# Attention scores of two heads in the two 64-row halves of TensorE, masks in VectorE's maxima, a padded last block

## The chip, the cores and the metric

One core of a Trainium2 chip runs the whole program. The metric is the device time of one execution in microseconds (us); several executions are timed and the median counts.

## The reference

Four sequences (B) of 576 positions (S) with eight heads (H) of 64 numbers (D) go through causal attention mixed with a memory read. The 2304 rows that come out are routed to eight experts of at most 288 rows each, and then go through a second feed-forward layer. The change touches the attention alone:

```
scores = scale * np.matmul(q, k.transpose(0, 1, 3, 2))      # q, k: (4, 8, 576, 64)
scores = np.where(causal, -1000000000.0, scores)
scores = scores - scores.max(-1, keepdims=True)
a = np.exp(scores)
a /= a.sum(-1, keepdims=True) + 1e-09
local = np.matmul(a, v)
...
mem_out = mem_ret / mem_norm
return (g * mem_out + (1 - g) * local).astype(np.float32)
...
x = np.ascontiguousarray(attn_out.transpose(0, 2, 1, 3)).reshape(B * S, H * D)
x = _moe_ref(x=x, **moe_kwargs)
return _moe2_ref(x=x, **moe2_kwargs)
```

## The kernel before, in words

The program has three stages, one after the other: attention, routing, and the experts with the second layer. Attention works on 16 pairs of heads (`pair(p)`: sequence `p // 4`, heads `2 * (p % 4)` and the next). Rows of 576 positions are cut into five blocks of 128, 128, 128, 128 and 64.

A number is held as a rounded high part and the low part that is left over, so that products come out nearly in full precision.

For each pair:

- Loads: K and Q with the 64 numbers of a head on partitions and both heads side by side (`Kr`, and `Qr`, which is loaded twice, into both halves of the partitions); Q in its natural layout, head 0 on partitions 0 to 63 and head 1 on 64 to 127 (`QN`); V, its transpose `VT`, and the memory `MZ`.
- Splitting: ScalarE casts `KX` (high), `QX` (high, twice) and `KB` (all of K); VectorE subtracts to get K's low part, into the lower half of `KX`, and Q's low part, `QL`. Each of these runs over 1152 columns.
- S, to find row maxima: `piece` multiplies a block of queries by the keys up to it (one matmul of 128 rows holds high and low parts of K), after a small matmul with `identb` and `mask_s` that puts a large negative number over the future keys (line 394 and then 396). For the last 64 queries, `QJ` holds both heads side by side with zeros between, and two matmuls (line 400) add up. VectorE reduces each piece to a maximum (line 413). These run about one pair ahead.
- nm: the ten columns of maxima are turned by a matmul (line 440), copied, and written by three small DMAs on ScalarE's queue (`fn3`, lines 449 and 450) into row 64 of `QL`.
- T, the scores again with keys on the output's partitions, so that they can feed the next product: `tprod` makes each block with two matmuls, K's high and low parts by Q's high part (line 555, 128 rows) and all of K by Q's low part with the row of minus the maxima (line 556, 65 rows). One head at a time; three groups of 512 columns a head, and the last 64 keys of both heads in a fourth group. ScalarE takes the exponential into `PT` (line 575), GpSimd zeroes the future keys on the diagonal (line 605).
- AV: `fAV` multiplies `PT` by V block by block into one buffer `av` (line 591), 15 blocks a head. In query block 4 the last product has 64 rows of `PT`. These matmuls are plain fp32, and each shows as two passes in the trace.
- mem (line 510) and the gate's product g0 (line 463) go through another single buffer; VectorE scales and adds (`norm`).

Beside this, 24 pieces of the last layer's weights are unpacked on ScalarE and VectorE (`conv`).

The order of the work on each engine is fixed when the program is built: `Plan.run` takes the tasks, each with a due number, an estimated length and the buffers it needs, and always places the task that can start first, by its estimates. Engines run their instructions strictly in that order, so an instruction that waits holds up all that stands behind it on its engine; DMA issues of SyncE's queue (SP) likewise. Rings limit how far things run ahead: S has three PSUM buffers, T two, `av` one.

Of the kernel before, what the change touches and what calls it, by code (L numbers as in the profile page):

```python
# [17 lines left out]
try:  # L18
# [36 lines left out]
BUFS = {"Kr": 2, "Qr": 2, "QN": 2, "MZ": 2, "V": 3, "VT": 2, "phi": 1, "ph": 1, "KX": 3, "QX": 3, "QL": 2, "KB": 2, "QJ": 2, "nm": 2,  # L55
        "nmt": 2, "PT": 2, "s": 3, "t": 2, "r5": 2, "tmp": 1, "rm": 2, "x": 2, "g": 2, "m2raw": 1, "m2a": 1, "m2b": 1}
OFFK = (0, 576, 1024, 1344, 1536)
MASK = -8.0e9
PRIO = {"load": -24, "prep": -18, "cb": 8, "S": -14, "ds": 1.2, "N": -5, "nmte": "ACT", "G": -3, "phi": -6, "mem": (1.6, 6.6), "memx": "ACT",
        "T": (0.5, 2.2, 3.5), "A": 5, "norm": 14, "gate": 6, "m2": (0.0, 6.3, 8.0), "tmg": (1, 6, 9, 12)}  # L60
VW, GW = 112, 112


C = 73
COLD, NLAT = 6000, 2600
# [32 lines left out]
class Ring:  # L98
    def __init__(self, n):
        self.n, self.made = n, []  # L100
# [14 lines left out]
class Plan:  # L115


    def __init__(self, cold=0):
        self.tasks, self.wrote, self.read, self.cold = [], {}, {}, cold
# [24 lines left out]
    def run(self):  # L144
# [7 lines left out]
        while len(order) < len(self.tasks):  # L152
            best, hold, cands = None, {}, []
            for t in ready:
# [7 lines left out]
                for e, c in t.engs.items():  # L162
# [7 lines left out]
                    st = max(at, free.get(e, 0), now)  # L170
# [58 lines left out]
def attention(g, tc, ctx, consts, beta, qT, kT, qN, v1, vT, mz, mT, wg, xd, L, m2):  # L229
# [10 lines left out]
    warm = cs.tile([128, 512], BF, name="warm")  # L240
    V.memset(warm, 0.0)
    zero = cs.tile([128, 192], F32, name="zero")
    G.memset(zero, 0.0)
    ms = cs.tile([128, 192], BF, name="mask_s")
    G.affine_select(ms[:, :128], zero[:, :128], pattern=[[-1, 128]], compare_op=OP.is_ge, fill=MASK, base=0, channel_multiplier=1)
    for i in range(2):
        q = slice(64 * i, 64 * i + 64)
        G.affine_select(ms[q, 128:], zero[q, :64], pattern=[[-1, 64]], compare_op=OP.is_ge, fill=MASK, base=0, channel_multiplier=1)
    identr = cs.tile([128, 128], F32R, name="identr")
    identb = cs.tile([128, 128], BF, name="identb")  # L250
    V.tensor_copy(identr, g.ident)
    V.tensor_copy(identb, g.ident)
# [7 lines left out]
    plan = Plan(COLD)  # L260
# [16 lines left out]
    def tile(name, shape, dt=F32):  # L277
        return (ld if name in ("Kr", "Qr", "QN", "MZ", "V", "VT") else wk).tile(shape, dt, name=name, bufs=BUFS[name])

# [12 lines left out]
    KB = [cs.tile([65, 2, S], F32R, name=f"KB{k}") for k in range(BUFS["KB"])]  # L292
    QJ = [cs.tile([128, 4, 64], F32R, name=f"qj{k}") for k in range(BUFS["QJ"])]
    for t in QJ:
        V.tensor_copy(t[:, 1:3].rearrange("p a b -> p (a b)"), zero[:, :128])
    tkb = []
    for k, t in enumerate(KB):
        def f(e, t=t):
            V.tensor_scalar(t[64:65, 0], warm[64:65, :256].bitcast(F32)[:, :1].to_broadcast([1, S]), 0.0, -1.0, op0=OP.mult, op1=OP.add)
            V.tensor_copy(t[64:65, 1], t[64:65, 0].bitcast(F32))  # L300

        tkb.append(add(10 * k - 7, {"DVE": 730}, f))
# [4 lines left out]
    def pair(p):  # L307
# [3 lines left out]
        bf = r.b = {x: Buf(R[x]) for x in ("Kr", "Qr", "QN", "MZ", "V", "VT", "phi", "ph", "KX", "QX", "QL", "KB", "QJ", "nm", "nmt",  # L311
                                           "PT", "av", "r5", "tmp")}
        parts = [(0, 1), (1, 2)] if p == 0 else [(0, 2)]
        k0 = n + W["load"]

        def load(name, shape, src, key, ns, a=None, z=None, dup=1, first=True):
            def f(e):
                if first:
                    setattr(r, name, tile(name, shape))
                t = getattr(r, name)  # L320
                for x in range(dup):
                    d = t[64 * x:64 * x + 64] if dup > 1 else t
                    nc.sync.dma_start(d if a is None else d[:, a:z], src if a is None else src[:, a:z])
            return add(key, {"SP": ns}, f, new=[bf[name]] if first else [], use=[] if first else [bf[name]])

        tK, tQ = [], []
        for u, (a, z) in enumerate(parts):
            tK.append(load("Kr", [64, 2, S], kT[b, pp], k0 - 3 * (p == 0) + .01 * u, 1400 // len(parts), a, z, 1, u == 0))
            tQ.append(load("Qr", [128, 2, S], qT[b, pp], k0 - 3 * (p == 0) + .011 * u + .001, 2200 // len(parts), a, z, 2, u == 0))
        tN = load("QN", [128, S], qN[b, pp], k0 + .1, 1200)  # L330
# [6 lines left out]
        tck, tcq, tsk, tsq, tcb = [], [], [], [], []  # L337
        for u, (a, z) in enumerate(parts):
            k, w = kp + .5 * u, S * (z - a)
            s = slice(a, z)  # L340

            def ck(e, s=s, u=u):
                if not u:
                    r.KX = tile("KX", [128, 2, S], F32R)
                copy(e, r.KX[:64, s], r.Kr[:, s])

            def cq(e, s=s, u=u):
                if not u:
                    r.QX = tile("QX", [128, 2, S], F32R)
                copy(e, r.QX[:, s], r.Qr[:, s])  # L350

            def sk(e, s=s):
                V.tensor_sub(r.KX[64:, s], r.Kr[:, s], r.KX[:64, s].bitcast(F32))

            def sq(e, s=s, u=u):
                if not u:
                    r.QL = tile("QL", [65, 2, S], F32R)
# [1104 lines left out]
```

## Time and profile before

| | us |
|---|---|
| median of 3 runs | 884.77 (881.39 to 887.12) |
| the profiled execution | 890.54, its span 888.8 |
| TensorE busy in the span | 842.4 (95%) |
| attention, to the last AV product | about 285 |
| routing | about 285 to 340 |
| experts and second layer | the rest |

The engines are TensorE (PE; PEld is its loading of weights), VectorE (DVE), ScalarE (ACT), GpSimd (POOL) and SyncE's queue (SP). A row of the timeline gives the start in us, the length, engine, line, operation, tile written <- tiles read, the weights' rows*columns, the shape of the moving data, and after x how many instructions or passes of one kind follow each other. TensorE overlaps neighbouring matmuls, so the length of one is not what it costs: the cost is from its start to the next one's start. A row of a line's instructions gives shortest/median/longest length in ns and then the first and the last start in us. A row of groups gives the line, the shapes and count, then the busy us and the mean ns of one.

### The profile page before, as it was taken

Reading aid. Unit: us, or ns where it says so; the run is one execution under the profiler, and the core shown is the slowest. Engines: PE = TensorE matmul, PEld = TensorE weight load, DVE = VectorE, ACT = ScalarE, POOL = GpSimd, SP = SyncE. Lnnn points to the kernel's source line nnn. Section 1 sums busy time; section 2 is a strip of 40 time slices with the busy share of each in tenths; the row PEclk is TensorE's granted clock in tenths of the full one; section 3 lists DMA queues with packets and bytes.
Section 4 is the critical chain, followed back from the end, with each engine's and each line's share of the span. In section 5 each row is a group of like instructions: output and inputs, shape, how many; then the busy total and the mean of one; then the engine's idle time right before and its main releaser. Section 6 shows DMA issues by size and latency. Waiting matters only on the chain.

```text
span 888.8 us, 17312 instructions
## 1 busy us (share of the span) xinstructions
PE 842.4 (95%) x6750; PEld 780.6 (88%) x6750; DVE 578.3 (65%) x1487; ACT 365.7 (41%) x826; POOL 96.8 (11%) x200
## 2 busy tenths in 40 slices
PE   8999999999998479979999999999999999999997
PEld 6888988888886379969999999999999999999996
DVE  7588888778874879957775775674586462542421
ACT  4667777667655223313412412412421432432311
POOL 1121112113111010113002002002001001000001
PEclk9999999999999579989999999999999999999999
DMA  8756776855630231252402421431330441430000
GB/s 215 176 153 178 222 200 183 227 159 163 186 93 24 92 108 49 81 113 68 149 25 69 127 47 52 143 49 48 133 72 28 142 73 30 140 72 25 25 1 37
DMA packets 39619, 92.87 MB, mean 104 GB/s; under 512 B 11184, under 2 KB 13360, under 8 KB 39536
## 3 DMA queue, kind: packets, MB, share of 16 engines
q1 hardware_dynamic: 36240, 82.24, 33.8%
q0 software_dynamic: 2976, 9.44, 3.2%
q8 instruction: 53, 0.87, 0.5%
q14 instruction: 30, 0.25, 0.1%
q10 hardware_dynamic: 320, 0.07, 0.0%
HBM read 82.21 MB, written 9.45 MB: 103 GB/s over the span
## 4 chain that ended last, share of the span: by engine, by line
PE 58%; issue 22%; DVE 5%; ACT 5%; DMA 4%; ACTq 2%; POOL 2%; SPq 1%; POOLq 0%; DVEq 0%
PE w L1204 8%; PE w L1206 8%; PE w L1205 8%; PE av L591 7%; PE acc L1205 4%; PE acc L1204 4%; PE acc L1206 4%; PE t L555 2%; PE mem L463 2%; DMA xg<-xd,tidx 2%; PE t L556 2%; PE s L396 2%; ACT x L533 2%; PE mem L510 2%; PE rps L953 1%
## 5 line engine op out<-in xcount | busy, mean ns | idle before, releaser
L1204 PE MATMUL w<-yh,mh 128*128 128x288 f32 x576 | 174.1, 302 | 0.0
L1206 PE MATMUL w<-yh,ml 128*128 128x288 f32 x576 | 169.9, 295 | 0.0
L1205 PE MATMUL w<-yl,mh 128*128 128x288 f32 x576 | 169.5, 294 | 0.0
L591 PE MATMUL av<-V,PT 128*128 128x112 f32 (+2 forms) x960 | 118.8, 263 | 1.3 <-DVE tmp L642 1.0
L591 PEld LDWEIGHTS av<-V,PT 128*128 128x128 f32 (+2 forms) x960 | 107.2, 173 | 8.9 <-issue 0.9
L1204 PEld LDWEIGHTS w<-yh,mh 128*128 128x128 f32 x576 | 108.8, 189 | 2.8
L1205 PEld LDWEIGHTS w<-yl,mh 128*128 128x128 f32 x576 | 108.5, 188 | 3.0
L1206 PEld LDWEIGHTS w<-yh,ml 128*128 128x128 f32 x576 | 108.4, 188 | 0.0
L1174 DVE TENSOR_TENSOR wlo<-wraw,whi 128x1024 fp32r<-128x1024 f32 x64 | 78.2, 1223 | 38.1 <-ACT whi L1170 38.1
L1311 DVE TENSOR_TENSOR mt<-w,mt 128x288 f32<-128x288 f32 x96 | 43.6, 455 | 81.6 <-PE w L1206 76.1
L1170 ACT CAST whi<-wraw 128x1024 fp32r<-128x1024 f32 x64 | 66.7, 1048 | 37.8 <-PE acc L1205 19.0
L413 DVE TENSOR_REDUCE nm<-s 128x1 fp32r<-128x512 f32 (+4 forms) x160 | 72.4, 475 | 14.5 <-PE s L400 6.4
L1205 PE MATMUL acc<-hl,whi 128*128 128x288 f32 x256 | 76.0, 297 | 1.4 <-DVE hl L1111 0.9
L1204 PE MATMUL w<-xhi,whi 128*128 128x288 f32 x256 | 77.2, 302 | 0.0
L1206 PE MATMUL w<-xhi,wlo 128*128 128x288 f32 x256 | 76.7, 299 | 0.1
L1205 PE MATMUL w<-xlo,whi 128*128 128x288 f32 x256 | 76.7, 300 | 0.0
L1072 ACT CAST gc<-mt 128x32 fp32r<-128x32 f32 (+2 forms) x72 | 17.5, 243 | 143.6 <-DVE mt L1311 138.9
L1204 PE MATMUL acc<-hh,whi 128*128 128x288 f32 x256 | 76.2, 297 | 0.0
L575 ACT ACTIVATE PT<-t 128x512 f32<-128x512 f32 x96 | 57.6, 601 | 43.5 <-PE t L556 28.6
L1206 PE MATMUL acc<-hh,wlo 128*128 128x288 f32 x256 | 75.2, 294 | 0.0
L1137 POOL DMA_INDIRECT xg<-xd,tidx x24 | 27.1, 1130 | 377.2 <-PE w L1206 181.5
L1111 DVE SCALAR_TENSOR_TENSOR hl<-w,hh 128x288 fp32r<-128x288 f32 x64 | 29.2, 456 | 59.0 <-ACT hh L1105 54.3
(219 smaller groups left out, 1802.9 us busy)
## 6 DMA issues: line engine op xcount, KB each, us to landing
wraw<-in_wr SPq DMA_DIRECT2D x64, 512.0 KB
Qr<-in_qT SPq DMA_DIRECT2D x30, 288.0 KB
m2raw<-in_m2w SPq DMA_DIRECT2D x12, 512.0 KB
V<-in_v SPq DMA_DIRECT2D x16, 365.0 KB
QN<-in_qN SPq DMA_DIRECT2D x16, 288.0 KB
VT<-in_vT SPq DMA_DIRECT2D x16, 288.0 KB
Kr<-in_kT SPq DMA_DIRECT2D x15, 288.0 KB
xd<-x SPq DMA_DIRECT2D x16, 256.0 KB
```

What stands on the lines that cost most here:

```text
L396: PE.matmul(d, r.QX[:, i, 128 * j:128 * j + 128], r.KX[:, i, a:z], start=False, stop=True, skip_group_check=True)
L413: V.tensor_reduce(r.nm[:, col:col + k], o.s[:, c:c + k * w].rearrange("p (k w) -> p k w", k=k), axis=AX.X, op=OP.max)
L575: A.activation(r.PT[:, items[0][0], out:out + 512], o.t, AF.Exp, scale=0.125)
L591: PE.matmul(AV[:m, i, j * C:j * C + w], r.PT[:kr, i, o:o + m], r.V[:kr, c:c + w], start=kb == 0, stop=kb == j)
L1111: V.scalar_tensor_tensor(lo(), src(), 0.0, hi().bitcast(F32), op0=OP.max, op1=OP.subtract)
L1137: g.gather = G.indirect_dma_start(out=x.xg[:96, c], out_offset=None, in_=xd, in_offset=bass.IndirectOffsetOnAxis(ap=r.tidx[:96, c:c + 1], ...
L1170: A.copy(x.W[fb][0], x.RAW[fb])
L1174: V.tensor_sub(x.W[fb][1], x.RAW[fb], x.W[fb][0].bitcast(F32))
L1204: nc.tensor.matmul(o, wh, rh, start=start, stop=False)
L1205: nc.tensor.matmul(o, wh, rl, start=False, stop=False)
L1206: nc.tensor.matmul(o, wl, rh, start=False, stop=stop)
L1311: V.tensor_max(q.mt, o.pt[:, :T], q.mt)
```

## The change

- K is loaded in its natural layout too (`KR`: head 0 on partitions 0 to 63, head 1 on 64 to 127), and `QN` serves for Q; `Qr` and `Kr` are gone. High and low parts `KH`, `QH`, `KL`, `QL` are tiles of 128 partitions by 576, so casts and subtractions have half the columns, and `KB` is gone.
- T of both heads is made together: each block has four products (`KH` by `QH`, `KL` by `QH`, `KH` by `QL`, and a constant of -1 by `NM`, which holds the maxima in rows 0 and 64), and each is issued for head 0 on rows 0 to 63 and at once for head 1 on rows 64 to 127, into two PSUM buffers. So there are eight matmuls where two heads had four. The last 64 keys go into the tail of the buffers that the third group's S takes.
- S uses high parts alone, both heads in the two halves; the mask's matmuls are gone. VectorE adds a mask while it takes the maximum (`tensor_tensor_reduce`, which is built as two instructions: the pass itself and one that writes out its accumulator). The last 64 queries take one matmul of 128 rows by 512 and one by 64.
- S of pair p+2 is issued behind T of pair p in the same task (`AHEAD = 2`); S and T share one ring of five PSUM buffers instead of three and two.
- The maxima get a cast of their own on ScalarE (`nmr`), and the DMAs that write them stand on SP's queue among the loads.
- AV goes query block by query block for both heads; `PT` has zeros in the missing 64 rows of its last block, so every AV product has 128 rows.
- `QJ` is copied by GpSimd.

```
-BUFS = {"Kr": 2, "Qr": 2, ..., "PT": 2, "s": 3, "t": 2, ...}
+BUFS = {"KR": 2, "QN": 3, ..., "PT": 2, "st": 5, ...}
...
-        for u, (a, z) in enumerate(parts):
-            tK.append(load("Kr", [64, 2, S], kT[b, pp], ...
-            tQ.append(load("Qr", [128, 2, S], qT[b, pp], ...
+        tK = load("KR", [128, S], kN[b, pp], k0 - 3 * (p == 0), 1200)
+        tN = load("QN", [128, S], qN[b, pp], k0 - 3 * (p == 0) + .001, 1200)
...
-                    if j < 4:
-                        PE.matmul(o.s[:, c + z - a - 128:c + z - a], identb, ms[:, :128], start=True, stop=False, ...)
-                        PE.matmul(d, r.QX[:, i, 128 * j:128 * j + 128], r.KX[:, i, a:z], start=False, stop=True, ...)
+                    for i in range(2):
+                        PE.matmul(o.s[i][:, c:c + 128 * j + 128], r.QH[H2[i], 128 * j:128 * j + 128], r.KH[H2[i], :128 * j + 128],
+                                  start=True, stop=True)
...
-                    V.tensor_reduce(r.nm[:, col:col + k], o.s[:, c:c + k * w].rearrange(...), axis=AX.X, op=OP.max)
+                        V.tensor_tensor_reduce(out=junk[:, :w], in0=o.s[x][:, c:c + w], in1=m, scale=1.0, scalar=-3.0e38, op0=OP.add,
+                                               op1=OP.max, accum_out=r.nm[:, col:col + 1])
...
-                A.dma_start(q[:, i, :512], r.nmt[4 * i:4 * i + 4])
-            A.dma_start(q[:, :, 512:], r.nmt[8:9].rearrange("o (i q) -> o i q", i=2))
+            nc.sync.dma_start(q[0:128:64, :512], r.nmt[:8])
+                nc.sync.dma_start(q[64 * i:64 * i + 1, 512:], r.nmt[8:9, 64 * i:64 * i + 64])
...
-                PE.matmul(d, r.KX[:, i, ks_], r.QX[:, i, a:z], start=True, stop=False)
-                PE.matmul(d, r.KB[:, i, ks_], r.QL[:, i, a:z], start=False, stop=True)
+                    for x, (wt, mv) in enumerate(((r.KH, r.QH), (r.KL, r.QH), (r.KH, r.QL), (None, r.NM))):
+                        for q, d in zip(H2, ts):
+                            PE.matmul(d[:kr, c:c + z - a], neg[q, :kr] if wt is None else wt[q, k], mv[q, a:z], start=x == 0, stop=x == 3)
...
-                    PE.matmul(AV[:m, i, j * C:j * C + w], r.PT[:kr, i, o:o + m], r.V[:kr, c:c + w], start=kb == 0, stop=kb == j)
+                    PE.matmul(AV[:m, i, j * C:j * C + w], r.PT[:, i, o:o + m], r.V[:, c:c + w], start=kb == 0, stop=kb == j)
```

On TensorE, S and T of a pair stood in small pieces between other work. Before, in the middle of attention (t is T, s with mask_s and identb is the mask, s<-KX,QX is S, mem is the memory):

```order
L440 MATMUL s<-identr,nm 9x128 [waits DVE_49]
L555 MATMUL t<-QX,KX 128x512 [waits Activation_49]
L556 MATMUL t<-QL,KB_126 128x512 [waits DMAHW7_49]
L394 LDWEIGHTS identb
L394 MATMUL s<-mask_s,identb 128x128
L396 MATMUL s<-KX,QX 128x512
L510 MATMUL mem<-MZ,phi 128x146
```

Now, at the end of T's second group and through the third (st is the shared ring; x2 is one matmul for each half):

```order
L557 MATMUL st<-nm_129,neg 128x448 x2
L384 MATMUL st<-KH,QH 128x384 [waits DVE_49] x2
L557 MATMUL st<-QH,KH 128x320 [waits Activation_49] x2
L557 MATMUL st<-QH,KL 128x320 x2
L557 MATMUL st<-QL,KH 128x320 x2
L557 MATMUL st<-nm_129,neg 128x320 x2
L557 MATMUL st<-QH,KH 128x192 x2
L557 MATMUL st<-QH,KL 128x192 x2
L557 MATMUL st<-QL,KH 128x192 x2
L557 MATMUL st<-nm_129,neg 128x192 x2
L557 MATMUL st<-QH,KH 64x64 [waits DVE_49]
L557 MATMUL st<-QH,KH 64x64 [waits Activation_49]
```

The work of 64 rows now stands in two runs a pair: the first group with its S, and the second and third groups with theirs, back to back. The third group's first matmuls wait for ScalarE, which empties the ring's buffers.

On SP's queue the loads and, now, the maxima's DMAs (nm_128<-nmt) stand in one row, behind loads that wait for buffers (m2raw is the weights' piece to unpack, which has one buffer):

```order
L324 DMA QN<-in_qN 128x576 [waits DMAHW6_49,DVE_49]
L324 DMA V<-in_v 128x730 [waits DMAHW7_49,PE_49]
L758 DMA m2raw<-in_m2w 128x1024 [waits DMAHW0_49,DMAHW3_49,DVE_49,Activation_49]
L439 DMA nm_128<-nmt 2x4x128 [waits DMAHW1_49,Activation_49]
L441 DMA nm_128<-nmt 1x16x4 [waits DMAHW2_49]
```

Before, SP's queue held loads alone in this place, and the three DMAs stood on ScalarE's queue.

On VectorE at the end of attention (L is the gate's sums, am the first step of routing), one unpacking now stands between the last sum and routing, where before there was nothing between them:

```order
L674 TENSOR_TENSOR L<-L,lt 64x8 [waits DVE_49]
L772 TENSOR_SCALAR m2b<-m2raw 128x512 [waits DMAHW4_49,DVE_49]
L775 SCALAR_TENSOR_TENSOR m2b<-m2a,m2b 128x512 [waits DVE_49,Activation_49]
L778 SCALAR_TENSOR_TENSOR w_80<-m2raw,m2b 128x512 [waits DVE_49]
L889 TENSOR_REDUCE am<-L 128x1 [waits Pool_49]
```

The three operations of the unpacking moved behind the last sum.

## Rows read from the trace of the kernel before

**Rows 1.** Stretch of nine pairs: its length, then each engine's busy us

```profile
64.90:211.30 146.40, 143.18 (x1134) 125.44 (x1134) 122.23 (x277) 103.33 (x241) 22.61 (x56) 1.00 0.68 193
```

**Rows 2.** Line 440, one matmul a pair: all of its matmuls

```profile
L440 PE MATMUL s<-identr,nm x16: 223/227/229, 14.4 to 260.5; 128*9 128x128 f32 x16
```

**Rows 3.** Line 555, T's first matmuls: all of them

```profile
L555 PE MATMUL t<-QX,KX x192: 191/302/502, 22.0 to 276.8; 128*128 128x512 f32 x32, 128*128 128x64 f32 x32, 128*128 128x448 f32 x32, 128*128 128x320 f32 x32
```

**Rows 4.** Timeline of TensorE through one pair

```profile
112.20 0.45 PE L555 MATMUL t<-QX,KX 128*128 128x512 f32 x1
112.48 0.39 PE L556 MATMUL t<-QL,KB 65*128 65x512 f32 x1
112.72 0.23 PE L394 MATMUL s<-mask_s,identb 128*128 128x128 bf16 x1
...
113.81 0.23 PE L394 MATMUL s<-mask_s,identb 128*128 128x128 bf16 x1
...
114.16 0.19 PE L555 MATMUL t<-QX,KX 128*128 128x64 f32 x1
...
114.79 2.38 PE L591 MATMUL av<-V,PT 128*128 128x112 f32 x20
117.01 0.22 PE L394 MATMUL s<-mask_s,identb 128*128 128x128 bf16 x1
...
117.30 0.31 PE L555 MATMUL t<-QX,KX 128*128 128x320 f32 x1
...
117.60 0.26 PE L555 MATMUL t<-QX,KX 128*128 128x192 f32 x1
...
117.90 0.99 PE L591 MATMUL av<-V,PT 128*64 128x73 f32 x10
...
119.81 0.23 PE L394 MATMUL s<-mask_s,identb 128*128 128x128 bf16 x1
...
120.24 0.65 PE L591 MATMUL av<-V,PT 128*128 128x112 f32 x4
...
123.11 0.35 PE L400 MATMUL s<-KX,qj 128*128 128x64 f32 x2
...
123.34 0.28 PE L555 MATMUL t<-QX,KX 128*128 128x64 f32 x1
123.46 0.28 PE L556 MATMUL t<-QL,KB 65*128 65x64 f32 x1
...
125.62 0.71 PE L400 MATMUL s<-KX,qj 128*128 128x512 f32 x2
126.17 0.31 PE L555 MATMUL t<-QX,KX 128*128 128x320 f32 x1
...
126.98 0.99 PE L591 MATMUL av<-V,PT 128*64 128x73 f32 x10
127.90 0.23 PE L440 MATMUL s<-identr,nm 128*9 128x128 f32 x1
```

**Rows 5.** Timeline: the first eight of the ten passes at 126.98

```profile
126.98 0.72 PE L591 MATMUL av<-V,PT 128*64 128x73 f32 x8
```

**Rows 6.** Timeline: the last two of them, with 64 rows

```profile
127.63 0.34 PE L591 MATMUL av<-V,PT 64*64 64x73 f32 x2
```

**Rows 7.** Timeline of line 713 in full, products into two halves of the columns

```profile
25.36 0.64 PE L713 MATMUL mem<-wb,m2raw 128*64 128x8 f32 x16
```

**Rows 8.** Groups of VectorE by shape, from 30 to 285 us

```profile
L413 DVE TENSOR_REDUCE nm<-s 128x1 fp32r<-128x512 f32 x42 | 28.7, 684 | 9.9 <-PE s L400 5.9 <-PE s L396 3.8
L353 DVE TENSOR_TENSOR KX<-Kr,KX 64x1152 fp32r<-64x1152 f32 x13 | 17.6, 1353 | 1.9 <-ACT KX L290 1.6
L436 DVE TENSOR_TENSOR nm<-nm 128x1 fp32r<-128x1 f32 x14 | 2.5, 178 | 0.3
```

**Rows 9.** The same for ScalarE

```profile
L575 ACT ACTIVATE PT<-t 128x512 f32<-128x512 f32 x92 | 55.2, 602 | 41.4 <-PE t L556 26.5 <-PE s L396 10.8 <-DMA QL<-nmt 4.0
```

**Rows 10.** Waits of SP's queue: us in total, times, longest

```profile
SPq L753 <- DVE w L773: 27.0, 14, 5.3
```

More of the change, by code (lines that the diff above doesn't have):

```diff
@@ L169, in run @@
                         at = max(at, u.end + (0 if u.eng == e else LAT[u.eng][e]))
-                    st = max(at, free.get(e, 0), now)
+                    st = max(at + self.wait * (e == "PE"), free.get(e, 0), now)
                     cands.append((t, e, c, st))
@@ new lines, in alone @@
+        def alone(o):
+            o.after(add(o.key, {"PE": o.cost + 130}, o.fn, o.deps, new=o.bs + o.first, use=o.use))
+        ks = n + W["S"]
+        r.pieces = [piece(ks + W["ds"] * a, [(j, 0)], [(i, 0, 128 * j + 128, 4 * i + j) for i in range(2)]) for a, j in enumerate((3, 2))]
+        r.pieces.append(piece(ks + W["ds"] * 2, [(1, 0), (0, 256)],
+                              [(i, c, w, 4 * i + j) for i in range(2) for j, c, w in ((1, 0, 256), (0, 256, 128))]))
+        if p < AHEAD:
+            for o in r.pieces:
+                alone(o)
@@ L559, in score @@
[L559 to L581 removed]
+        ex, mk = {}, {}
@@ L618, in pair @@
[L618 to L622 removed]
+                m = rows(kb)
+                v = r.PT[:m, :, OFFK[kb]:OFFK[kb] + m]
+                G.affine_select(v, v, pattern=[[0, 2], [1, m]], compare_op=OP.is_ge, fill=0.0, base=0, channel_multiplier=-1)
@@ new lines, in select @@
+            gi = (0, 1, 2, 2, 3)[kb]
+            mk[kb] = add(n + W["T"][min(gi, 2)] + .1 + .01 * kb, {"POOL": 100 + 2.5 * rows(kb)}, f, [ex[0, gi], ex[1, gi]], use=[bf["PT"]])
+        outs = []
+        for gi in range(3):
+            score(gi)
+        for kb in range(NJ):
+            select(kb)
+        for j in range(NJ):
+            for i in range(2):
+                need = [mk[x] for x in range(j + 1)] + ([ex[x, 1] for x in range(2)] if j == 4 else [])
+                outs.append(add(n + W["A"][j] + .5 * i, {"PE": (225, 450, 675, 900, 330)[j]}, fAV(i, j),
+                                need + outs[-2:][:1] * (j > 0) + [r.tV] + (fill if p == 0 else []), new=[bf["av"]] if not outs else [],
@@ L721, in attention, with begin @@
         tmg.append(add(W["tmg"][b] + .1, {"ACT": 156}, f1, [t], use=[bm]))
+    ahead, gens = {}, {}
+    def begin(p):
+        if p < NP:
+            gens[p] = pair(p)
+            ahead[p] = next(gens[p])
+    for p in range(AHEAD):
+        begin(p)
     for p in range(NP):
-        r = pair(p)
+        begin(p + AHEAD)
+        r = next(gens[p])
         b, pp = divmod(p, H // 2)
```

328 lines of the change are left out of this document (146 added, 182 removed).

## The prediction

> **What bounds the kernel now.** I read the busy times by stretch first. Over nine pairs in the middle of attention TensorE is busy for 143.2 of 146.4 us, VectorE for 122.2 (83%) and ScalarE for 103.3 (71%) [rows 1]: TensorE's queue sets the pace, at 146.4 / 9 = 16.3 us a pair. The rows of line 440, one matmul a pair, tell the same over nearly all of attention: 15 steps from 14.4 to 260.5, 16.4 us each [rows 2]. So a microsecond taken off TensorE's queue in one pair is worth 16 at the end, as long as nothing else falls behind. Attention ends with a chain of small steps into routing, and the later stages share nothing with the change, so I move them by whatever attention gains.
>
> Then I read one pair in the timeline, always from start to start [rows 4]. T of one head: the first group takes 0.52 (112.20 to 112.72), the second 0.63 (114.16 to 114.79), the third 0.60 (117.30 to 117.90), or 0.81 with the last 64 keys of both heads behind it (126.17 to 126.98). Two heads: 2 x (0.52 + 0.63) + 0.60 + 0.81 = 3.71. S with its masks: 0.35 for 512 columns (113.81 to 114.16), 0.29 for 384 (117.01 to 117.30), 0.43 for 256 and 128 together (119.81 to 120.24), each for two heads, and 0.23 (123.11 to 123.34) and 0.55 (125.62 to 126.17) for the last queries: 2.92. T and S are 6.63 us of a pair.
>
> **The change on TensorE.** First the price of one matmul when the next follows at once [rows 4]: 0.24 for 512 columns (112.48 to 112.72), 0.15 for 320 (two in 117.30 to 117.60), 0.12 for 64 (123.34 to 123.46; here the load of 128 columns of weights sets it). Between these I put 0.21 for 448, 0.18 for 384, 0.13 for 256 and 0.12 for 192 and 128. With 64 columns of weights: eight passes last 0.72, of which the last one's own length is about 0.22; seven steps in 0.50 make 0.07 [rows 5].
>
> If the two halves run side by side, a couple of matmuls costs what one does. T: 4 products x (0.24 + 0.12 + 0.21 + 0.15 + 0.12 + 0.07) = 3.64, about what it was. S: 0.24 + 0.18 + 0.13 + 0.12 = 0.67, and the last queries 0.28 + 0.12 = 0.40, half of what they were. Together 4.71. That a couple costs one is not shown for rows by any row of before. The nearest is line 713, whose products alternate between the two halves of the columns: sixteen passes with 64 columns of weights last 0.64, so fifteen steps take 0.42, 0.028 each [rows 7], against 0.071 in one half [rows 5]. There two halves did run at once, weights included. I take that end; the other, one after the other, is a rival.
>
> Here a measured figure of the Trainium skill ("TensorE: Matmul & The Clock Gate", Part 3, "Measured speedup vs the span model") speaks against full overlap. It gives 3.07 times for four row tiles of 512 columns, not 4; by that a couple would cost 1.30 of one, 4.31 x 0.30 x 16 = 21 us more over attention. No row here has row tiles, and line 713 shows no such loss; the rule is weighed as a rival below.
>
> Going from 128 rows to 64 and back has a price. Ten even passes of 0.071 would take 0.71; with 64 rows in the last two (they begin at 127.63 [rows 6], the next work at 127.90) the ten take 0.92 [rows 4], so 0.21 for in and out. The new order has two runs of 64 rows a pair: 0.42. At the entry the first load of weights is not hidden: the first 512-column matmul of a group takes 0.28 (112.20 to 112.48) and not 0.24, twice 0.04. T and S become 4.71 + 0.42 + 0.08 = 5.21, a gain of 1.42.
>
> The padded last block makes those two switches of AV vanish, once for each head: 2 x 0.21 = 0.42.
>
> **The new wait.** T's third group now follows the second at once, and its first matmuls wait for ScalarE to empty buffers of the ring. One exponential takes 0.60 [rows 9]; the S of 384 columns in between covers 0.18. Below: 0, if the buffer is free by chance. Above: 1.2, both exponentials in a row. I take 0.5, one exponential less its cover and something for the hand-over. Behind the waiting matmul stand the rest of T, this pair's AV and all of TensorE's queue.
>
> Net for one pair: 1.42 + 0.42 - 0.5 = 1.34; for sixteen 21.4 us.
>
> **The other engines.** VectorE loses two subtractions of 1152 columns (1.35 each) for two of 576 (about 0.68 by the 512-column reduction), -1.3 a pair; its nine masked maxima each get an instruction that writes one column, between 0 and the 0.18 of the smallest operation, up to +1.6 a pair [rows 8]. I price the masked pass itself like the reduction of the same columns. VectorE's 122.2 / 9 = 13.6 us a pair [rows 1] become 12.3 to 13.9, against 16.3 - 1.3 = 15.0 for TensorE: hidden, with little room. ScalarE sheds three casts of 1152 columns for two of 576 and three DMA issues, and gets a small cast and a second copy; at 71% busy nothing of it shows. GpSimd is busy for 22.6 of 146.4 [rows 1]; its copies of `QJ` are hidden there.
>
> On SP the maxima's three DMAs stand behind loads. The unpacking's loads waited 27.0 us in 14 times for their buffer, the longest 5.3 [rows 10]. But the maxima of a pair are turned before the second run of the pair ahead of it and are used in the next first run, over half a pair, some 8 us, later. I cost it at nothing; if a wait of 5.3 came on top of copying and landing in every pair, the excess would stop T's fourth product and with it TensorE.
>
> **Start and end.** T first starts at 22.0 us [rows 3]. S now needs no low parts, and Q comes once. But pair 0's T is followed on TensorE by S of pair 2, whose loads are issued behind pair 0's maxima. I take 2 us, between 0 and 5. At the end one unpacking stands between the last sum and routing's first reduction: three operations of 512 columns, about 0.68 each [rows 8], 2 us; 0 if it runs earlier. The two cancel.
>
> **The sum.** 21.4 us. From the profiled execution's 890.5 that gives 869; this execution was 5.8 above the median, and I take the same off the median: 884.8 - 21.4 = 863.4, say 863. With the wait at 0 and 5 us at the start: 16 x 1.84 + 5 = 34, 850. With the wait at 1.2: 16 x 0.64 = 10, 875.
>
> **The rivals.**
>
> 1. The halves run one after the other. Every couple costs two: T and S's 4.31 once more, less some 0.3 of the new wait that longer S covers, 4.0 x 16 = 64 us: 863 + 64 = 927, slower by 5%. Against it stands line 713 [rows 7]; for it, that no row shows halves of rows. It decides alone: above 1 + 21.4 / (4.31 x 16) = 1.31 of one matmul for a couple, nothing is gained.
> 2. They overlap in part, because the second half's load of weights comes behind the first's. Then 0.12 shows where few columns cover it, about 0.1 in four of T's six blocks: 4 x 0.36 = 1.4, and 0.2 in S, 1.6 x 16 = 26 us: 889, no change. Line 713 loads in both halves without loss [rows 7], which speaks against it. The Trainium skill's 3.07 of 4, named above, would end in about the same place, 884.
> 3. The couples overlap, but the ring of five buffers or VectorE, at about 87%, holds TensorE up at more places: for each run one reduction of 0.68 late, 1.4 a pair instead of part of my 0.5, about 1 us more: 863 + 16 = 879. If the masked pass took twice the reduction's time, VectorE itself would need over 16 us a pair, and this would end at no change.
> 4. The change does not do what it says, since T costs the same and most of S was hidden. I see no cover: TensorE is busy 98% [rows 1], so S's time is on the path.
>
> **Chances.** The forecast, 850 to 875: 0.68. Quicker, with no wait and a better start: 0.05. Rival 3: 0.12, a third of it below 876. Rival 2: 0.08. Rival 1: 0.07. A measurement of this kernel can tell about 1%, 9 us, from no change. Faster by more than that (below 876) is 0.68 + 0.05 + 0.04 = 0.77; within 1% the rest of rival 3 and most of rival 2, 0.15; slower 0.08. For the range I leave out rival 1, half of rival 2 and what is quicker than 848: 848 to 884 holds about 0.8.
>
> **What would show it.** Right: the matmul of the maxima recurs every 15 us; T's and S's matmuls come in couples a few ns apart and the couple with 512 columns takes 0.24; one wait of TensorE for ScalarE of about half a microsecond a pair; the AV products of query block 4 take 0.71 and not 0.92. Wrong: couples at 0.4 or more for 512 columns (rivals 1 and 2); TensorE idle for VectorE or for the maxima's DMA several times a pair, or VectorE above 95% (rival 3); T starting later than 22 us.

## The result and the profile after

| | before | changed | ratio, 95% interval |
|---|---|---|---|
| median of the comparison | 885.94 (4 runs) | 873.61 (871.64 to 874.77, 4 runs) | 0.9872 [0.9831, 0.9913] |
| again, beside e2 to e4 (e1) | 886.23 (13 runs) | 872.44 | 0.9823 [0.9764, 0.9882] |
| again, beside e13 to e15 (e16) | 887.84 (7 runs) | 874.78 | 0.9853 [0.9827, 0.9879] |
| the profiled execution | 890.54, span 888.8 | 874.77, span 873.0 | |

The kernel became faster by 12 to 14 us. Forecast were 22 us, to 863.0; the time lies inside the range of 848 to 884, and a little over half of the gain came.

In the rows below, st is a buffer of the ring that S and T share, pt the exponentials' tile, KH, KL, QH and QL the high and low parts, junk the output of the masked maximum that nobody reads. The first view is the stretch of nine pairs in the middle, which answers [rows 1], and the matmul of the maxima, which answers [rows 2]:

```profile
59.90:197.80 137.90, 131.74 (x1253) 114.33 (x1252) 109.52 (x352) 85.52 (x248) 26.44 (x72) 1.00 0.52 159
```

```profile
L430 PE MATMUL st<-identr,nmr x16: 227/228/319, 16.7 to 243.3; 128*9 128x128 f32 x16
```

A pair takes 137.9 / 9 = 15.3 us and not 16.3. TensorE's share fell from 98% to 96%: something waits now. VectorE has 12.2 us of work in a pair, ScalarE 9.5.

The timeline of TensorE, as in [rows 4], first a piece with T's first group and the last column block of AV, then the second and third group:

```profile
133.45 0.50 PE L557 MATMUL st<-QH,KH 64*128 64x512 f32 x2
133.79 0.39 PE L557 MATMUL st<-QH,KL 64*128 64x512 f32 x2
134.03 0.40 PE L557 MATMUL st<-QL,KH 64*128 64x512 f32 x2
134.26 0.39 PE L557 MATMUL st<-nm,neg 64*128 64x512 f32 x2
134.49 0.40 PE L384 MATMUL st<-KH,QH 64*128 64x512 f32 x2
134.82 0.85 PE L597 MATMUL av<-V,pt 128*64 128x73 f32 x10
135.60 1.01 PE L504 MATMUL mem<-MZ,phi 128*128 128x146 f32 x6
```

```profile
121.67 0.36 PE L557 MATMUL st<-QH,KL 64*128 64x448 f32 x2
121.87 0.36 PE L557 MATMUL st<-QL,KH 64*128 64x448 f32 x2
122.07 0.37 PE L557 MATMUL st<-nm,neg 64*128 64x448 f32 x2
122.28 0.33 PE L384 MATMUL st<-KH,QH 64*128 64x384 f32 x2
122.45 0.31 PE L557 MATMUL st<-QH,KH 64*128 64x320 f32 x1
123.89 0.41 PE L557 MATMUL st<-QH,KH 64*128 64x320 f32 x1 [1.14 <-ACT pt L583]
```

Each "x2" is a couple, one product for each head. From start to start a couple of 512 columns costs 0.23 to 0.24, of 448 columns 0.20, of 384 0.17: what one matmul cost before. The ten passes of AV's last column block take 0.78 (134.82 to 135.60), before 0.92. And here the second matmul of the third group starts 1.44 behind the first: it waits for ScalarE. Every pair has such a wait, and this is the longest: TensorE's idle time there is 1.14 in this pair and 0.36 to 0.87 in the others. ScalarE's timeline at that place:

```profile
122.01 1.34 ACT L527 ACTIVATE x<-mem,rm 128x64 f32<-128x64 f32 x6 [0.73 <-DVE g L517]
123.21 1.12 ACT L583 ACTIVATE pt<-st 128x512 f32<-128x512 f32 x2
```

The two exponentials that free the buffers stand behind six evictions of mem. Over all pairs the waits of TensorE (total, times, longest) put 9.0 us there, those of its weight loads 12.9:

```profile
PE st L557 <- ACT pt L583: 9.0, 14, 1.1
```

```profile
PEld st L557 <- ACT pt L583: 12.9, 14, 1.4
```

VectorE's groups by shape from 30 to 267 us, which answer [rows 8]: the masked maximum of 512 columns takes 690 ns, as long as the plain one (684) in [rows 8], and writing its accumulator out 83 each time.

```profile
L397 DVE CUSTOM_DVE_ANT_0 junk<-st,mask 128x512 bf16<-128x512 f32 x26 | 17.9, 690 | 13.3 <-PE st L384 11.9
L397 DVE DVE_READ_ACCUMULATOR2_ANT nm<- 128x1 f32 x124 | 10.3, 83 | 0.0
```

The start. T first runs at 25.2 us, before at 22.0 [rows 3]. TensorE, then ScalarE, then SP's queue:

```profile
23.47 1.80 PE L504 MATMUL mem<-MZ,phi 128*128 128x146 f32 x6 [2.31 <-issue]
25.20 0.79 PE L557 MATMUL st<-QH,KH 64*128 64x512 f32 x2
```

```profile
22.43 0.67 ACT L294 CAST KH<-KR 128x576 fp32r<-128x576 f32 x1 [1.66 <-DMA KR<-in_kN]
23.00 0.37 ACT L294 COPY mg<-mem 64x32 f32<-64x32 f32 x2
```

```profile
17.33 0.67 SPq L439 DMA_DIRECT2D nm<-nmt  x1
18.05 1.24 SPq L441 DMA_DIRECT2D nm<-nmt  x2
19.40 0.52 SPq L324 DMA_DIRECT2D KR<-in_kN  x1
```

Read from the end: TensorE's mem products need the single buffer that the copy of mg at 23.00 empties (the row names no releaser; this follows from the kernel, and e2 below tests it). That copy stands on ScalarE behind the cast of pair 2's K; the cast waits for the load, and the load went out at 19.40, behind the DMAs of pair 0's maxima. TensorE idles for 2.3 us, and its clock falls behind it (the column behind POOL is the granted clock; 0.50 is the lower of its two levels, 1.2 GHz):

```profile
20.00:25.00 5.00, 2.40 (x23) 2.11 (x23) 1.55 (x2) 2.31 (x8) 1.15 (x4) 0.77 0.86 267
25.00:30.00 5.00, 4.26 (x24) 3.33 (x24) 1.96 (x7) 2.36 (x8) 0.41 (x1) 0.50 0.28 104
30.00:35.00 5.00, 5.00 (x44) 3.76 (x41) 1.95 (x8) 3.55 (x9) 0.82 (x3) 0.70 0.16 34
```

The end. Between the last sums on VectorE and routing's first reduction (L889) stand three operations of the unpacking:

```profile
270.28 0.43 DVE L772 TENSOR_SCALAR m2b<-m2raw 128x512 int32<-128x512 int32 x1
270.81 0.69 DVE L775 SCALAR_TENSOR_TENSOR m2b<-m2a,m2b 128x512 int32<-128x512 int32 x1
271.54 0.69 DVE L778 SCALAR_TENSOR_TENSOR w<-m2raw,m2b 128x512 int32<-128x512 int32 x1
272.15 0.29 DVE L889 TENSOR_REDUCE am<-L 128x1 f32<-128x144 f32 x1
```

### The profile page after: what moved, and what is told of

The parts are those of the page before. It is cut to its first block, busy times and chain, and to the rows that moved or that the text cites. A ratio compares the mean times of both kernels' runs of the same rounds, so it can differ in the third digit from the quotient of the medians.

```text
span 873.0 us, 17954 instructions
## 1 busy us (share of the span) xinstructions
PE 820.9 (94%) x6958; PEld 760.7 (87%) x6958; DVE 559.1 (64%) x1628; ACT 334.5 (38%) x839; POOL 100.7 (12%) x234
## 4 chain that ended last, share of the span: by engine, by line
PE 68%; issue 22%; DVE 4%; ACT 3%; DMA 2%; POOL 2%; POOLq 0%; DVEq 0%; ACTq 0%
PE av L597 12%; PE w L1209 9%; PE w L1211 8%; PE w L1210 8%; PE st L557 6%; PE acc L1210 4%; PE acc L1209 4%; PE acc L1211 4%; PE mem L504 3%; PE mem L456 2%; DMA xg<-xd,tidx 2%; PE rps L958 1%; ACT x L527 1%; PE st L384 1%; PE av L689 1%
## 5 line engine op out<-in xcount | busy, mean ns | idle before, releaser
L597 PE MATMUL av<-V,pt 128*128 128x112 f32 (+1 forms) x960 | 111.8, 265 | 0.0
L597 PEld LDWEIGHTS av<-V,pt 128*128 128x128 f32 (+1 forms) x960 | 98.2, 173 | 12.9 <-issue 8.5
L397 DVE CUSTOM_DVE_ANT_0 junk<-st,mask 128x512 bf16<-128x512 f32 (+2 forms) x144 | 66.2, 460 | 30.1 <-PE st L384 20.4
L583 ACT ACTIVATE pt<-st 128x512 f32<-128x512 f32 x96 | 52.4, 605 | 25.1 <-PE st L557 24.2
```

The lines of the kernel that those rows point to most:

```text
L397: V.tensor_tensor_reduce(out=junk[:, :w], in0=o.s[x][:, c:c + w], in1=m, scale=1.0, scalar=-3.0e38, op0=OP.add, op1=OP.max, accum_out=r.nm ...
L583: A.activation(r.PT[:, i, 512 * gi:512 * gi + 512], o.t[i], AF.Exp, scale=0.125)
L597: PE.matmul(AV[:m, i, j * C:j * C + w], r.PT[:, i, o:o + m], r.V[:, c:c + w], start=kb == 0, stop=kb == j)
```

## The experiments

My theory after reading the traces: the couples do run at once, and the missing gain went to the start, to the wait for the ring, and to a padding that is worth less than forecast. The rivals: that VectorE or the ring's depth holds TensorE whatever ScalarE's order, that the start is bound by the maxima's transfers, and that the halves' overlap is not where T's gain comes from. Pair lengths below are those of the 13 pairs from the third to the sixteenth matmul of the maxima.

**e1: the changed kernel again**, beside the next three.

> The changed kernel once more, to set the size of the effect on a chip that runs the other kernels of this call beside it. Theory A (the two profiles differ by 15.8 us, of which 4.6 us are the profiled execution of before being above its median): ratio 0.985 to 0.989, about 12 us. Theory B (the profiles tell the true effect): 0.981 to 0.983, about 16 us.

872.44, ratio 0.9823 [0.9764, 0.9882]; a pair takes 15.30 us, and T starts at 25.1. The effect on this chip is 13.8 us by the medians, between the two theories and less than the 15.8 between the profiled spans. The interval spans both theories, so e1 doesn't decide between them.

**e2: pair 2's K and Q loaded earlier.**

```
-        tK = load("KR", ..., k0 - 3 * (p == 0), 1200)
+        tK = load("KR", ..., k0 - 3 * (p == 0) - 8 * (p == 2), 1200)
```

(and the same for `QN`.)

> The changed kernel with the loads of pair 2's K and Q issued on SP ahead of the beta, m2raw and first-row-maxima transfers instead of behind them; nothing else is changed. Theory A: the start lost about 5 us to the forecast since mem(0) waits for a copy on ScalarE that stands behind the cast of KR(2), whose load was issued only at 19.4 us; then the first T stands at 21 to 23 us instead of 25.2, TensorE's idle stretch 21.2 to 23.5 goes, and the time falls 3 to 6 us against the changed kernel. Rival: the first T is bound by the row maxima's transfers (nm), which the two loads now delay; T stays at 25 or moves later and the time is the same within 1 us or 1 to 3 us longer.

867.35 beside 872.44, 5.1 less; ratio 0.9775 [0.9719, 0.9831]. TensorE at the start, and the clock:

```profile
22.20 0.64 PE L708 MATMUL mem<-wb,m2raw 128*64 128x8 f32 x16 [0.52 <-ACT mg L294]
22.77 0.63 PE L557 MATMUL st<-QH,KH 64*128 64x512 f32 x2
```

```profile
25.00:30.00 5.00, 4.88 (x39) 4.04 (x39) 3.10 (x11) 3.12 (x10) 0.88 (x4) 0.86 0.60 220
30.00:35.00 5.00, 5.00 (x54) 4.57 (x52) 2.51 (x13) 3.73 (x12) 2.14 (x5) 1.00 0.07 18
```

T starts 2.4 us earlier, the low stretch is shorter, and the third matmul of the maxima comes at 40.4 instead of 44.2. Of the 2.4 us, 1.7 come from the planner, which with this edit puts pair 0's mem behind T's first group (at 25.04, in the changed kernel ahead of it at 23.47); the 3.7 us at the third matmul of the maxima are the fairer measure. The pairs stay at 15.31. So the start did cost 4 to 5 us, and through the place of two loads; that the maxima's transfers hold it falls, as these went out 0.1 later here. e15, below, repeats it.

**e3 and e6: the exponentials ahead of mem's evictions on ScalarE**, in the changed kernel (e3) and with the early loads (e6). In the sorted list of tasks, those evictions are moved behind the second group's exponentials:

```
+        for t in [t for t in seq if hasattr(t, "evict")]:
+            a = seq.index(t)
+            z = next((k for k in range(a + 1, min(a + 13, len(seq))) if hasattr(seq[k], "second")), None)
...
+            seq.insert(z, seq.pop(a))
```

> The changed kernel with the two exps of T's second group moved ahead of the six evictions of the second half of mem on ScalarE's queue, in 11 or more of the 16 pairs; nothing else is changed. Theory A: the ring wait in T's third group (0.8 to 1.1 us a pair) is set by those evictions, 1.34 us, that stand in front of the exps; the wait falls below 0.3 and the time falls by 0.6 to 0.9 us a pair, 8 to 13 us in all. Rival B: the wait moves on to g0, which then waits for the later evictions to free MEM; the wait in T falls but as much appears in front of g0, and the time stays within 3 us. Rival C: VectorE is what holds the ring; the wait in T stays.

> The kernel with the two early loads (e2), and the exps of T's second group ahead of the mem evictions as in e3. In e3 the pairs grew shorter by 0.16 us each, but the clock of the start rose later and took 2 us back. Theory A (what e3 lost was the clock of its start alone): no low stretch after 35 us, pairs of 15.14 us, and 1.5 to 3 us less than the kernel with the early loads, which was 0.9775 of before: 0.974 to 0.976. Rival B (exps first delays what stands behind it): the same as e2 within 1 us, 0.977 to 0.979.

e3 gave 873.58, no gain (e1: 872.44); e6 871.09, ratio 0.9796 [0.9742, 0.985]. The wait in T's third group fell in e3:

```profile
PE st L567 <- ACT pt L593: 5.5, 13, 0.4
```

But 0.4 of it stays in each pair; one exponential lasts 0.55. Pairs took 15.14 in both, 0.16 less, which makes some 2.5 us over sixteen. At the start it was lost again: the clock stood at 0.50 in e3 from 30 to 35 us, where the changed kernel had 0.70, and in e6 from 25 to 30, where e2 had 0.86, and the third matmul of the maxima came 2.0 and 1.8 us later. That this is the edit's doing isn't shown: in e16, the changed kernel again, the clock stood at 0.50 from 30 to 35 too, and that matmul came at 46.3, as in e3 (46.2). The medians can't tell 2.5 us from this. So theory A of e3 holds for the place, with a quarter of its size a pair; the evictions are the lesser part of the wait.

**e4: the padding alone, in the kernel before.**

```
-                    PE.matmul(AV[...], r.PT[:kr, i, o:o + m], r.V[:kr, c:c + w], ...)
+                    PE.matmul(AV[...], r.PT[:, i, o:o + m], r.V[:, c:c + w], ...)
```

with two fixed tiles for `PT` whose last rows are zeroed once.

> The kernel before with the padding alone: PT in two fixed buffers whose lower half of the last block is zeroed once, and AV's last block taken with 128 rows instead of 64. Theory A (the forecast's): the two switches between 128 and 64 rows per pair and head go, 0.42 us a pair, 6 to 7 us in all. Theory B (by the traces of the changed kernel, where the ten passes of the last column block take 0.78 us instead of 0.92): 0.28 us a pair, 4 to 5 us in all. Rival: the static PT takes a release order away and costs as much as it gains; within 2 us of before.

884.95 beside 886.23, ratio 0.9979 [0.9953, 1.0006]; a pair 16.31 instead of 16.37. The ten passes took 0.78 instead of 0.92, twice a pair, but TensorE waited more often for mem's evictions in front of the gate products: 5.7 us in 11 times, before 4.0 in 8. All its waits together grew from 0.36 to 0.53 a pair.

```profile
PE mem L466 <- ACT x L536: 5.7, 11, 0.9
```

**e11 and e14: the padding undone, with the early loads** (`r.PT[:rows(kb), ...]` and `r.V[:rows(kb), ...]` again).

> The kernel with the two early loads (e2), with AV's last key block taken with 64 rows again as in the kernel before. Theory A (as e4 showed in the kernel before: 0.15 us of AV and 0.07 us of the pair): 1 to 3 us more than e2, and the ten products of the last column block 0.92 instead of 0.78 us. Theory B (the forecast's 0.42 us a pair holds in the changed kernel): 6 to 7 us more.

> The kernel of e11 once more, beside e2's on the same chip. Theory A (the padding is worth what the pairs show, 0.28 us each): 4 to 5.5 us more than e15. Theory B (the 877 us of e11 hold): 8 to 10 us more.

e11 came to 877.06 on another chip, ratio 0.9924 [0.9891, 0.9956] against e2's 0.9775, which is more than either of its theories had; its six runs scatter from 872 to 882. e14 came to 875.48 beside 871.01 for e15, the early kernel on the same chip: 4.5 us more, as its theory A had it. In e11's trace a pair takes 15.59 instead of 15.31, all of it AV (6.65 us a pair instead of 6.37). So the padding is worth 0.28 us a pair where TensorE's queue is full, and nearly nothing in the kernel before, where it ran into the next wait. This is read from the pairs, which are the same in both traces but for one; that the medians of e14 and e15 differ by the same is in part luck, since the medians hold the clock too. In e14's profiled execution the longest of the waits for ScalarE (1.13; the others 0.37 to 0.86) was followed by ten us at the lower clock, and that pair lasted 20.5 us. The same pair of e11 has the same wait and kept its clock. Such stretches may be why the runs scatter (872 to 878 in e14); only one execution of each has a trace.

```profile
120.00:122.00 2.00, 0.87 (x9) 0.56 (x7) 1.86 (x7) 2.00 (x8) 0.00 (x0) 0.95 0.94 319
122.00:132.00 10.00, 10.00 (x57) 8.88 (x55) 4.17 (x17) 4.11 (x11) 1.68 (x4) 0.50 0.17 53
```

**e5, e10 and e9: is it the halves?** e5 issues a block's four products of half 0, then the four of half 1; e10 all products of a group of half 0, then all of half 1 (4, 8 and 8 in the three groups, not 4, 8 and 12 as expected below); e9 takes both heads from rows 0 to 63.

```
-                    for x, (wt, mv) in enumerate(...):
-                        for q, d in zip(H2, ts):
+                    for q, d in zip(H2, ts):
+                        for x, (wt, mv) in enumerate(...):
```

> The changed kernel with T's loops exchanged: a half's four products of a column block are issued one behind the other, and then those of the other half, where the changed kernel issues the same product of both halves next to each other; products, results and buffers are the same. Theory A (the couples run side by side because they are issued next to each other, and T gains from that alone): couples of a 512-column product go from 0.23 to 0.46 us, and T's three groups and the last block from some 4.0 to 7.5 us a pair: 3 to 3.7 us a pair, 48 to 59 us in all, 920 to 932 us. Rival: the two halves overlap whatever their order, or T has slack: within 5 us of the changed kernel.

> The changed kernel with T's halves farther apart than in e5: all products of half 0 of a group, then all of half 1: 4, 8 and 12 products in a row in T's three groups and 4 in its last block. Theory A (one half runs ahead of the other by any number of products that the queue holds, at least 12): the groups take what they took, pairs of 15.3 us, within 2 us of e5, 876 to 879. Theory B (it runs ahead by a few products, 4 to 7): the second and third group come apart in part, 0.3 to 1.2 us a pair, 5 to 19 us more, 880 to 895.

> The changed kernel with the scores of both heads taken from rows 0 to 63 alone (head 1's scores are made from head 0's keys and queries, so head 1's result is not the reference's); the number of products, their sizes, banks and order stay. Theory A (T and the scores are cheap because a couple runs in the two halves of the rows at once; in e5 the order did not matter since the halves run ahead of each other by themselves): couples become two products one behind the other, 0.46 us for two of 512 columns, T and scores go from 5.5 to some 8.5 to 9.5 us a pair, and the last AV stands 45 to 66 us later, 917 to 938 us in all. Rival (something else holds T, so that half of its products are hidden anyway): within 10 us of the changed kernel.

e5: 876.82 (2 runs; ratio 0.9867 [0.9796, 0.9937], on a chip where before had 889.66); e10: 872.59 (one run). Pairs of 15.31 and 15.33, so theory A of e5 is wrong: the order in the program does not matter. In e5's timeline the couples are couples still:

```profile
124.60 0.47 PE L557 MATMUL st<-QH,KH 64*128 64x448 f32 x2
124.88 0.39 PE L557 MATMUL st<-QH,KL 64*128 64x448 f32 x2
```

In e10 half 0 has begun the third group's first product (320 columns) when half 1 begins its last one of the second (448), though the program has them the other way round:

```profile
120.94 0.33 PE L384 MATMUL st<-KH,QH 64*128 64x384 f32 x1
121.01 0.36 PE L558 MATMUL st<-QL,KH 64*128 64x448 f32 x1
121.11 0.31 PE L558 MATMUL st<-QH,KH 64*128 64x320 f32 x1
121.21 0.36 PE L558 MATMUL st<-nm,neg 64*128 64x448 f32 x1
```

e9: 973.84 (one run), 101 us more than e10 on the same chip. On the same rows a couple of 512 columns costs 0.46 instead of 0.23:

```profile
134.26 0.62 PE L557 MATMUL st<-QH,KL 64*128 64x512 f32 x2
134.72 0.63 PE L557 MATMUL st<-QL,KH 64*128 64x512 f32 x2
```

A pair takes 21.4 us, 6.1 more. T, S and the last queries have 4.2 of it, AV 1.0, the gate products 0.6, mem 0.3. AV and the gate products were not touched; they got longer because the clock fell in this stage as well, to 0.50 for 7 to 14 us at a time:

```profile
118.25:131.75 13.50, 13.45 (x60) 12.32 (x60) 5.79 (x23) 5.18 (x13) 1.59 (x4) 0.50 0.36 126
133.00:143.00 10.00, 10.00 (x71) 8.36 (x70) 6.23 (x18) 3.93 (x15) 0.55 (x2) 1.00 0.34 114
```

Five of the pairs kept the full clock. They take 18.5 to 19.2, on average 3.4 more than the same pairs of the changed kernel, all of it in T (7.4 instead of 4.6) and S (1.5 instead of 0.85); AV, the gate products and mem are there what they were. So the gain of T and S does come from the two halves at once, and what theory A of e9 left out is the clock, which makes nearly half of the 6.1.

**e7 and e12: S of 384 columns out of T's second group**, so that the third group finds two of the five buffers free; both with the early loads. Its products and maxima are put behind the gate products (e7), or behind the last queries and the third group's maxima (e12):

```
-                if s:
+                if s and gi != 1:
                     s.fn(e)
```

> The kernel with the two early loads (e2), and the products of the next scores with 384 keys taken out of T's second group and put behind the gate products, with their two maxima behind them; ScalarE's order is as in the changed kernel. T's third group then takes the third and fourth of the five buffers and waits for none. Theory A (the ring's depth is what holds the third group): the wait in T falls from 0.65 us a pair to under 0.1, the products that were moved pay one more switch between 64 and 128 rows, 0.2 to 0.4, and pairs shorten by 0.25 to 0.45 us: 4 to 7 us less than with the early loads, 0.970 to 0.973 of before. Rival B: the wait goes to the moved products or to the last queries behind them, which now need the buffers of the third group's exps: the same within 2 us.

> As e7, but the moved scores with 384 keys stand behind the last queries, and their two maxima behind those of the third group, so that the exps of the last block, the copy of V behind them and mem do not wait for them. Theory A (in e7 the saved ring wait came back as the wait of mem for V's copy, because the maxima of the moved scores stood ahead on VectorE): T's wait under 0.1 us a pair, no wait at mem, pairs of 14.9 to 15.1 us and 3 to 6 us less than e2. Rival B (the saved time comes back in yet another wait, or the switches eat it): pairs of 15.2 us or more, within 2 us of e2.

e7: 873.23, ratio 0.9816 [0.9757, 0.9875], pairs of 15.33. T's share of a pair fell from 4.64 to 3.80, but AV's rose from 6.37 to 6.92 and six times mem waited 1.0 us for the copy of V, which on ScalarE now stood behind exponentials that VectorE held up:

```profile
129.23 0.91 PE L516 MATMUL mem<-MZ,phi 128*128 128x146 f32 x4 [1.09 <-ACT V L303]
```

e12, with the maxima in a better place: **862.41** (861.49 to 862.69), ratio 0.9746 [0.9719, 0.9773], faster than both kernels. Pairs of 14.78, 0.53 less. T's third group begins without a wait:

```profile
115.79 0.37 PE L569 MATMUL st<-nm,neg 64*128 64x448 f32 x2
116.00 0.30 PE L569 MATMUL st<-QH,KH 64*128 64x320 f32 x2
116.14 0.31 PE L569 MATMUL st<-QH,KL 64*128 64x320 f32 x2
```

T's share fell by 0.87 a pair (4.64 to 3.77), and 0.22 of it went into the switches of the moved S (0.85 to 1.07), another 0.12 into its neighbours. TensorE's idle time alone fell from 0.64 to 0.07 a pair; the rest of the 0.87 the trace doesn't count as idle. So the ring's depth held TensorE for 0.87 us a pair, rival 3 of the forecast in a milder form, and the cure is in the order of work.

**e8 and e13: the unpacking earlier**, with two raw buffers, added to e2 (e8) and to e12 (e13).

```
-"m2raw": 1, ... "m2": (0.0, 6.3, 13.5)
+"m2raw": 2, ... "m2": (0.0, 5.6, 10.0)
```

> The kernel with the two early loads (e2), and the unpacking of the second layer's weights with two raw buffers in place of one and its pieces due earlier, so that the last piece is unpacked on ScalarE and VectorE inside the last pair instead of behind it; the planner also places pieces of the middle otherwise. Theory A (the unpacking stands on VectorE ahead of the routing's first reduction and costs its 1.9 us at the end): 1.5 to 2.5 us less than with the early loads, 0.975 to 0.976 of before. Rival B: the routing's first product waits for the last pair's sums and not for the unpacking, or the pieces cost as much inside the pairs: the same within 1 us, 0.977 to 0.979.

> The early loads (e2), the late scores (e12) and the second raw buffer with earlier pieces (e8) together. Theory A (the unpacking ahead of the routing is real time at the end): 1.5 to 2.5 us less than e12's 862.4, 860 to 861. Rival (what it frees at the end it costs in the pairs): 862 to 865.

e8: 867.35, ratio 0.9777 [0.9718, 0.9836], as e2. In its trace routing's first product comes 3.99 us behind the last AV product, in e2 5.78, so the end is 1.8 shorter; the median does not show it. e13: 871.34, 9 more than e12: the planner's other places for the unpacking made pairs of 10 to 23 us; in one of them nearly two idle us of TensorE were followed by ten at the lower clock, and a second stretch of seven came later. That the unpacking costs 1.8 us at the end is shown by the trace; that it can be had back is not.

**e15 and e16: early and changed kernel once more**, beside e14.

> The kernel of e2 once more, beside the changed kernel on the same chip: 866 to 869 us, 3 to 6 us less than e16.

> The changed kernel once more, on the chip that runs the others of this call: 871 to 874 us by its runs so far.

871.01 and 874.78, both above what was expected, on a chip where before had 887.84; 3.8 us less by the early loads. Ratios 0.9817 [0.9795, 0.984] and 0.9853 [0.9827, 0.9879]. The third matmul of the maxima came at 40.3 and 46.3.

## Why the prediction was right in direction and wrong in size

Of the 22 us that were forecast some 12 came. Two steps failed. The start was priced with T 2 us earlier, and T came 3.2 later: a miss of 5.2 us. And the ring's wait was put at 0.5 a pair where the runs show 0.87: 5.9 us over sixteen pairs. The padding was mis-sized (0.28 a pair for 0.42), and some 4 us of the miss stood in the base that the forecast was taken off.

**What bounds the kernel: right.** TensorE's queue set the pace, and nothing else took over: VectorE came to 12.2 us a pair, forecast were 12.3 to 13.9, and its masked pass cost what a reduction costs. The maxima's DMAs on SP's queue, costed at nothing, cost nothing: no wait of TensorE for them shows.

**The couples: right, and near the forecast in size.** T with S took 7.03 us a pair before, over the 13 pairs, masks and all waits included, and takes 5.83 now. Without the ring's 0.87 that is 4.96, 2.07 less. Some 0.37 comes back at the neighbours, where the switches between 64 and 128 rows show: mem 0.11, the maxima 0.09, the gate products 0.02, and AV 0.15 (6.65 unpadded in e11, 6.50 before). Net 1.7; the forecast had 1.42. But not all of it is the couples'. TensorE waited 0.36 a pair in before, 0.25 of it in front of the gate products for mem's evictions, and the changed kernel has none of these waits; the forecast took no account of them. Without them 1.34 is left, and 0.34 of that are the nine matmuls of the masks, which the forecast counted in S. The 3.07 of 4 in the Trainium skill ("TensorE: Matmul & The Clock Gate", Part 3, "Measured speedup vs the span model") did not show for two halves: a couple of 512 columns costs 0.23 to 0.24, one alone cost 0.24. Rivals 1 and 2 fall; e9 shows what rival 1 would have cost: 3.4 a pair at the full clock, where the forecast had 4.0, and another 2.7 by the clock.

**The padding: the mechanism right, the size wrong.** I took ten even passes at 0.071, 0.71, from 0.92 and called the rest the price of the switch. Even with 128 rows throughout they take 0.78. So 0.14 a head and not 0.21, 0.28 a pair and not 0.42 (e11, e14). The 0.071 was read between passes of one kind; from the last of them to other work it takes 0.16 even with 128 rows. The ten steps are now 0.12 for the first, 0.06 to 0.07 for each of the next eight and 0.16 for the last, 0.78 in all.

**The ring's wait: in the place named, and 0.87 instead of 0.5.** My step had one exponential less its cover. It left out ScalarE's queue: six evictions of mem (1.34 us, at 122.01) stand ahead of the exponentials. e3 shows that they make about a quarter of the wait; the rest is the depth of five buffers, as e12 shows.

**The pair in sum.** Forecast 1.42 + 0.42 - 0.50 = 1.34; the runs show 1.70 + 0.28 - 0.87 = 1.11, and the pairs' own lengths 16.37 - 15.30 = 1.07.

**The start: wrong in mechanism.** I saw that pair 2's loads are issued behind pair 0's maxima, and priced T 2 us earlier all the same. T came 3.2 later, which is one of the signs that the forecast had named for being wrong: a miss of 5.2. The step followed T's own inputs and not the queue in front of it: ScalarE's in-order queue carried the wait for a load of pair 2 over to a copy that pair 0's mem needs, and the idle 2.3 us were followed by ten at a lower clock. e2 and e15 give 5.1 and 3.8 back.

**The end: right in kind.** Two us were forecast for the unpacking, and it takes 1.9 (270.28 to 272.15). From the last AV product to routing's first product it is 2.96 before and 5.78 in e1, 2.8 more. The other 0.9 wasn't in the forecast: VectorE's sums for head 0 of the last pair began 4 us ahead of the last AV product in before (280.8 and 284.8), and now, with AV going block by block for both heads, both heads' sums begin behind it (267.07).

**The balance.** From T of pair 0 to T of pair 15 the traces differ by 19.8 (22.0 to 268.6 before, 25.2 to 252.0 after), and 15 x 1.34 = 20.1 was forecast. That these agree is luck: the 13 steady pairs gave 15.0 and not 17.4; the first two gave 4.8 and not 2.7, where before too had a low clock, 0.66 from 30 to 35 us. With the start's 5.2 and 0.8 of the end the forecast is short by 6.3 us at routing: 15.1 in place of 21.4. The other 4 are in the base. The median of before was 885.9 beside the changed kernel, not 884.8, which is 1.2 of them. And I took a difference of traces off a median: before's profiled execution lies 4.6 above its median there, the changed kernel's 1.2, so the spans differ by 15.8 and the medians by 12.3. Where that comes from is open: from routing's first product to the end the two profiled executions took 601.0 and 600.5, the others 596.6 to 600.3, so only 0.5 of the difference lies there, and no other execution of before has a trace.

## What to carry to other kernels

Follow an early load through every in-order queue that stands between it and the first use of something else: a cast that waits for pair 2's data stopped pair 0. Where two uses share one ring of buffers, count the buffers between an allocation and the release that it needs, and move what takes buffers ahead of a waiting group to behind it, instead of making the release faster. A removed microsecond on the bounding engine counts only as far as the next wait: the padding was worth 0.28 us a pair in one kernel and 0.07 in the other.

## What the chip showed that I had not expected

- Matmuls on the two halves of TensorE's rows started out of the program's order: with half 1 issued four, or eight, products behind half 0 the pairs took the same 15.3 us (e5, e10). For them it doesn't hold that an engine runs its instructions strictly in the program's order, as the section on the kernel before says of all engines. The median lag between the two of a couple in T's first two groups was 3 ns in the changed kernel and 13 to 23, by width, in e5.
- When all T and S products stood on the same 64 rows, TensorE was busy throughout and the granted clock still fell to 0.50 for 7 to 14 us at a time (e9). With the halves side by side it stayed at 1.00 through the nine pairs in the middle.
- One pair of the changed kernel has a wait of 1.13 us, the longest of its waits for ScalarE. In e14 it was followed by ten us at the lower clock, at a price of 5 us; in the changed kernel, e11 and e15 the same wait in the same pair was followed by nothing. What made that execution different is open.
